# First head of an attention kernel prepared in two halves, with its hash bits in one bank

## The chip, the cores and the metric

The kernel runs on one core of a Trainium2 chip. The metric is the device time of the whole program in microseconds (us), the median of several executions. The engines are TensorE (PE in the rows, its weight loads PEld), VectorE (DVE), ScalarE (ACT), GpSimd (POOL) and SyncE (SP), which here only issues DMAs.

## The reference, cut to what matters

Four batches of eight heads, 768 positions, 64 values to a position. Six random projections give each query and key six sign bits; a query sees only the keys with the same bits. The result goes through a feed-forward layer of 3072 tokens.

```python
q_bits = (einsum('bhsd,dk->bhsk', q, proj) > 0); k_bits = (einsum('bhsd,dk->bhsk', k, proj) > 0)
q_bucket = sum(q_bits * 2**arange(6)); k_bucket = sum(k_bits * 2**arange(6))
scores = where(q_bucket == k_bucket, (q @ k.T) / sqrt(D), -1e9)
attn = exp(scores - max(scores)); attn = attn / (sum(attn) + 1e-9)
x = (attn @ v) reshaped to 3072 x 512
h = x @ w_in
g = where(h >= 1, h, where(h <= -1, 0, (h + 1)**2 / 4))
out = g @ w_out
```

## The kernel before

Every float32 operand is split into a rounded high part and the low remainder, each in an `fp32r` tile, and products are sums of matmuls over the parts. Two heads make a pair. Three buffers `T1[i]`, `T2[i]` hold a pair's q and k: high parts, low parts and, in eight rows of `T2`, the hash bits as large signed numbers (rows 0 to 6) and the negated, clamped row maxima (row 7), so that the score matmuls add mask and maximum by themselves. `sub` (L39) makes a low part: raw minus high.

Each of the 32 heads is 12 units `g` (two halves of the 768 queries by six blocks of 128 keys). A unit is two score matmuls (`s_unit`, L297 and L298), two exponentials on ScalarE (L306 rounded, L311 full), one subtraction for the low part `pl` (`lo_unit`; on GpSimd for key blocks 0 and 3, so in units 0, 3, 6 and 9 of a head, else on VectorE), and, four units later, three matmuls with v (`pv_unit`, L330 to L332). Beside them the maxima of a coming head are made: per block of 128 queries two matmuls into the one PSUM tile `smax` (`max_mm`, L258) and one reduce on VectorE (`max_red`, L262). As there is one such tile, TensorE and VectorE take it in turn. Then `max_clamp` (L269, L271), a transpose on TensorE (`max_tr`, L276), and `max_put`: a copy to `te` on ScalarE and two DMAs, into row 7 (L282) and into the scratch tensor `ed` (L283).

The bits of a coming pair come from four matmuls with the projection `pw` into an output bank (`bits_mm`, L178), a negated copy on ScalarE, a comparison on VectorE (`bits_cmp`, L189), a scaling on GpSimd (`bits_scale`, L221) and four DMAs (`bits_put`, L230). `move` (L157) copies q's and k's parts between partitions by DMA; `load_raw`, `load_v`, `cast_v` and `split_v` bring a pair's inputs and split v.

The order on each engine is the order of the code; `tasks[g]`, filled by `at(g, ...)`, holds the side work of unit g. Before unit 0 the first pair is prepared directly, without moves: `prep_direct` (L161 cast and four L39 subtractions on VectorE for head 0, on GpSimd for head 1, three copies on ScalarE), `bits_direct` (one bank, one negation and one comparison per half and per q or k), then `max_pre`, 12 score matmuls (L356) each with a reduce (L359). `keep_busy` puts matmuls into the program whose result nobody reads: 28 of them, 16 of 384 columns and 12 of 128.

## Time and profile before

| | us |
|---|---|
| median of three runs | 1021.12 (1020.1 to 1021.44) |
| profiled execution | 1021.61 |
| span in its trace | 1019.6 (2.0 lie around it) |
| TensorE busy in the span | 993.9 |
| VectorE, ScalarE, GpSimd busy | 696.6, 647.5, 395.0 |

A row of a timeline has start and duration in us, then engine, line, operation, tile written and tiles read; in brackets stands how long the engine had been idle and what released it. Tiles are given without their buffer number, so `t` stands for any part of `T1` or `T2`. "L258 of head 2" is the `max_mm` for the third head; it is the first work in the program that needs the second pair's tiles.

### The profile page before, as it was taken

What the parts mean: (1) busy time and instruction counts of PE and PEld (TensorE: products, weight loads), DVE (VectorE), ACT (ScalarE), POOL (GpSimd) and SP (SyncE); (2) the same over time, 40 slices, a digit from 0 to 9 for tenths busy, and PEclk for the clock granted to TensorE, in tenths of its full rate; (3) what the DMA queues carried; (4) which work ended last, traced back from release to release, by engine and by line L of the source; (5) the groups of instructions that cost most, each with busy time, mean ns of one, the idle gap of its engine ahead of it and who ended that gap; (6) DMA issues with size and microseconds to landing.
All of it is one profiled execution on the core that took longest, in us unless ns stands there. A gap on an engine that the chain in (4) does not pass through costs nothing.

```text
span 1019.6 us, 15241 instructions
## 1 busy us (share of the span) xinstructions
PE 993.9 (97%) x5180; PEld 917.5 (90%) x5180; DVE 696.6 (68%) x1108; ACT 647.5 (64%) x1430; POOL 395.0 (39%) x458
## 2 busy tenths in 40 slices
...
GB/s 89 167 110 155 160 171 174 182 169 169 158 171 153 152 141 144 127 107 180 63 80 88 50 32 79 47 22 81 24 77 48 1 79 47 32 71 24 32 1 32
DMA packets 52229, 99.06 MB, mean 97 GB/s; under 512 B 12856, under 2 KB 33976, under 8 KB 52152
## 3 DMA queue, kind: packets, MB, share of 16 engines
...
q14 instruction: 36, 0.29, 0.1%
q10 hardware_dynamic: 216, 0.00, 0.0%
...
## 4 chain that ended last, share of the span: by engine, by line
PE 89%; DVE 5%; ACT 2%; DMA 1%; issue 1%; SPq 0%; POOL 0%; DVEq 0%; ACTq 0%
PE y L638 26%; PE h L600 25%; PE smax L258 7%; PE o L332 6%; PE s L298 6%; PE o L330 6%; PE o L331 6%; PE s L297 6%; PE o L178 2%; DVE nm L262 1%; DMA wsq<-wd 1%; DVE nm L359 1%; DVE pl L39 0%; ACT ph L306 0%; DMA pj_raw<-in_pj_dram 0%
## 5 line engine op out<-in xcount | busy, mean ns | idle before, releaser
L607 DVE SCALAR_TENSOR_TENSOR t<-t 128x384 f32<-128x384 f32 x128 | 73.0, 571 | 257.6 <-ACT z L606 257.5
L605 ACT ACTIVATE t<-h,mh 128x384 f32<-128x384 f32 x128 | 74.3, 581 | 267.4 <-PE h L600 266.2
L306 ACT ACTIVATE ph<-s 128x384 fp32r<-128x384 f32 x380 | 188.1, 495 | 46.9 <-PE s L298 40.6
L262 DVE TENSOR_REDUCE nm<-smax 128x1 f32<-128x768 f32 x186 | 176.2, 947 | 19.9 <-PE smax L258 18.4
L39 POOL TENSOR_TENSOR pl<-pf,ph 128x384 fp32r<-128x384 f32 x128 | 137.9, 1083 | 81.2 <-ACT pf L311 80.8
L39 DVE TENSOR_TENSOR pl<-s,ph 128x384 fp32r<-128x384 f32 x256 | 135.5, 544 | 15.3 <-ACT s L311 14.0
L550 POOL TENSOR_TENSOR xraw<-xraw,xr 128x384 f32<-128x384 f32 x24 | 30.2, 1258 | 272.2 <-DVE xraw L547 272.2
L297 PE MATMUL s<-t 128*128 128x384 f32 x384 | 132.0, 344 | 0.8 <-DVE t L212 0.8
L332 PE MATMUL o<-pl,va 128*128 128x386 f32 x384 | 130.4, 339 | 0.4 <-DVE pl L39 0.3
L298 PE MATMUL s<-t 128*128 128x384 f32 x384 | 130.2, 339 | 0.0
L330 PE MATMUL o<-ph,va 128*128 128x386 f32 x384 | 130.1, 339 | 0.0
L331 PE MATMUL o<-ph,vb 128*128 128x386 f32 x384 | 129.5, 337 | 0.0
L311 ACT ACTIVATE s<-s 128x384 f32<-128x384 f32 x252 | 125.3, 497 | 0.0
L600 PE MATMUL h<-t,wih 128*128 128x384 f32 x480 | 122.7, 336 | 0.0
L638 PE MATMUL y<-t,ghi 128*128 128x512 f32 x384 | 120.2, 394 | 0.0
L258 PE MATMUL smax<-t 128*128 128x384 f32 x372 | 101.5, 353 | 5.4 <-DVE nm L262 4.5
L600 PEld LDWEIGHTS h<-t,wih 128*128 128x128 f32 x480 | 88.0, 188 | 4.9
L258 PEld LDWEIGHTS smax<-t 128*128 128x128 f32 x372 | 63.9, 188 | 22.1 <-DVE nm L262 21.1
L606 ACT ACTIVATE z<-t,m 128x384 f32<-128x384 f32 x128 | 79.0, 617 | 4.1
L638 PEld LDWEIGHTS y<-t,ghi 128*128 128x128 f32 x384 | 71.4, 188 | 11.2
L600 PE MATMUL h<-t,wil 128*128 128x384 f32 x240 | 80.8, 337 | 0.0
L638 PE MATMUL y<-t,glo 128*128 128x512 f32 x192 | 76.3, 398 | 2.9 <-DVE glo L627 2.9
...
## 6 DMA issues: line engine op xcount, KB each, us to landing
...
```

The lines of the kernel that those rows point to most:

```text
L39: eng.tensor_tensor(out=out, in0=a, in1=b, op=ALU.subtract)
L258: nc.tensor.matmul(out=smax[hd][:, hf, 0:HS], lhsT=t2[:, 0, h, i * P:(i + 1) * P], rhs=t2[:, 1, h, hf * HS:(hf + 1) * HS], start=True, sto ...
L262: nc.vector.tensor_reduce(out=nmp(hd)[:, i:i + 1], in_=smax[hd][:, :, 0:HS], axis=AX.XY, op=ALU.max, negate=True)
L297: nc.tensor.matmul(out=ps[:, 0:HS], lhsT=t1[:, 1, h, ks], rhs=t1[:, 0, h, sl], start=True, stop=False)
L298: nc.tensor.matmul(out=ps[:, 0:HS], lhsT=t2[:, 1, h, ks], rhs=t2[:, 0, h, sl], start=False, stop=True)
L306: nc.scalar.activation(out=ph[:, 0:HS], in_=ps[:, 0:HS], func=AF.Exp, scale=SCALE)
L311: nc.scalar.activation(out=pf, in_=ps[:, 0:HS], func=AF.Exp, scale=SCALE)
L330: nc.tensor.matmul(out=o, lhsT=wa, rhs=ph, start=(jj == 0), stop=False)
L331: nc.tensor.matmul(out=o, lhsT=wb, rhs=ph, start=False, stop=False)
L332: nc.tensor.matmul(out=o, lhsT=wa, rhs=pl, start=False, stop=(jj == NJ - 1))
L600: nc.tensor.matmul(out=ps[:, 0:CH], lhsT=w[:, cs], rhs=x[:, ct, :], start=(n == 0), stop=(n == 3 * NCT - 1))
L638: nc.tensor.matmul(out=ys[c][m], lhsT=g_[:, ms], rhs=w, start=(f == 0 and k == 0), stop=(f == NFT - 1 and k == 2))
```

## The change

The first head is cast, split and turned into bits in two halves of 384 columns, loaded by two DMAs (`hi_low`, `hi_copy`). q's and k's bits of a half lie in one bank (`direct_mm`), with one negation and one comparison for both on 40 rows. Head 1's raw data is loaded ahead of v. GpSimd's clearing of tiles stands first in its queue, but for T2[2], which it clears in unit 8. Eight of ten copies into `pw` go to units 1 and 2; `cast_v(0)` stands ahead of the exponentials. The first head's maxima are put in two halves (`half_max`, `half_clamp`, `half_put`). Eleven unread matmuls are left (five of 384 columns, six of 128). Head 1's maxima run in units 2 to 7 where they ran in 1 to 6; the second pair's bits are put in unit 9, behind `max_put`, where they were put in unit 8 ahead of it. In the changed kernel the lines are L305 and L306 for the score matmuls, L266 and L270 for the maxima, L284 for the transpose, L290 and L291 for `te` and L238 for the bits.

```diff
+    def hi_low(h, raw, eng, hf):
+        t1, t2 = T1[0], T2[0]
+        sl = slice(hf * HS, (hf + 1) * HS)
+        eng.tensor_copy(out=t2[:, 1, h, sl], in_=raw[:, sl])
+        sub(nc, eng, t1[64:128, 1, h, sl], raw[64:128, sl], t2[64:128, 1, h, sl].bitcast(F32))
+        sub(nc, eng, t1[0:64, 0, h, sl], raw[0:64, sl], t2[0:64, 1, h, sl].bitcast(F32))
+    def hi_copy(h, raw, sl, which):
+        t1, t2 = T1[0], T2[0]
+        out, rows = ((t1[0:64, 1], slice(64, 128)), (t1[64:128, 0], slice(0, 64)),
+                     (t2[64:128, 0], slice(0, 64)))[which]
+        nc.scalar.copy(out=out[:, h, sl], in_=raw[rows, sl])
...
+    def direct_mm(h, hf, ps):
+        direct[hf] = ps
+        sl = slice(hf * HS, (hf + 1) * HS)
         for t in (1, 0):
...
+            nc.tensor.matmul(out=ps[:, 0:HS], lhsT=pw[:, 3 - t, :], rhs=T1[0][:, t, h, sl],
+                             start=(t == 1), stop=(t == 0))
...
+    def direct_cmp(h, hf):
+        ps = direct[hf][0:40, 0:HS]
+        nc.vector.tensor_tensor(out=ps, in0=ps, in1=direct[h, "neg"][:, hf * HS:(hf + 1) * HS], op=ALU.is_gt)
+    def direct_scale(h, t, hf, eng):
+        rows = slice(0, 8) if t else slice(32, 40)
+        ps, out = direct[hf][rows, 0:HS], T2[0][0:8, t, h, hf * HS:(hf + 1) * HS]
...
+    def half_max(q, i, hf, ps):
+        t2 = T2[0]
+        n = q * HT + i
+        nc.tensor.matmul(out=ps[:, 0:HS], lhsT=t2[:, 0, 0, n * P:(n + 1) * P],
+                         rhs=t2[:, 1, 0, hf * HS:(hf + 1) * HS], start=True, stop=True)
+        return lambda: nc.vector.tensor_reduce(out=half[q][0][:, hf, i:i + 1], in_=ps[:, 0:HS], axis=AX.X,
+                                               op=ALU.max, negate=True)
+    def half_clamp(q):
+        a, nm = half[q]
+        nc.vector.tensor_reduce(out=nm[:, 0:HT], in_=a.rearrange("p f i -> p i f"), axis=AX.X, op=ALU.min)
...
+    def half_put(q, ps):
+        k = (1 + 2 * q) * HT
+        nc.tensor.transpose(out=ps[0:k, 0:P], in_=half[q][1], identity=ident)
+        te = small.tile([k, P], F32R, name=f"te{q}", bufs=1)
+        nc.scalar.copy(out=te, in_=ps[0:k, 0:P])
+        nc.sync.dma_start(out=T2[0][7:8, 0, 0, q * HS:(q + 1) * HS].bitcast(F32), in_=te[0:HT, :].bitcast(F32))
+        if q == 1:
+            nc.sync.dma_start(out=e_d[0][0:1, :], in_=te[HT:k, :].bitcast(F32))
...
+    for sl in (H0, H1):
+        nc.sync.dma_start(out=first[0][:, :, sl], in_=qk[0][:, 0:1, sl])
...
+    nc.sync.dma_start(out=first[1], in_=qk[0][:, 1:2])
     load_v(0)
-    nc.sync.dma_start(out=first[1], in_=qk[0][:, 1:2])
     load_raw(1)
-    nc.vector.memset(pw.bitcast(F32), 0.0)
-    nc.vector.memset(T2[0][0:64, 0].bitcast(F32), 0.0)
-    for i in (1, 2):
-        nc.gpsimd.memset(T2[i][0:64, 0].bitcast(F32), 0.0)
+    nc.vector.memset(pw[:, 2:4].bitcast(F32), 0.0)
+    nc.vector.memset(T2[0][0:64, 0, 0].bitcast(F32), 0.0)
     make_identity(nc, ident)
+    for t, x in [(t, 1.0) for t in VA] + [(t, 0.0) for t in VB]:
+        nc.gpsimd.memset(t[:, :, 1].bitcast(F32), x)
+    for t, x in [(t, 1.0) for t in PH] + [(t, 0.0) for t in PL]:
+        nc.gpsimd.memset(t[:, HS:HS + 2].bitcast(F32), x)
+    nc.gpsimd.memset(T2[0][0:64, 0, 1].bitcast(F32), 0.0)
+    nc.gpsimd.memset(pw[:, 0:2].bitcast(F32), 0.0)
+    nc.gpsimd.memset(T2[1][0:64, 0].bitcast(F32), 0.0)
     nc.scalar.copy(out=pj_hi, in_=pj_raw)
     nc.vector.tensor_tensor(out=pj_raw, in0=pj_raw, in1=pj_hi.bitcast(F32), op=ALU.subtract)
...
+    def pw_put(i, rows, c, low=32):
         nc.scalar.copy(out=pw[rows, i, c:c + NB], in_=pj_hi[rows].bitcast(F32))
-        nc.scalar.copy(out=pw[rows, i, 32 + c:32 + c + NB], in_=pj_raw[rows])
...
+    pw_put(2, slice(0, 128), 0, 64)
+    pw_put(3, slice(0, 128), 32, 64)
+    for hf, sl in ((0, H0), (1, H1)):
+        hi_low(0, raw, nc.vector, hf)
+        for n in range(2):
+            hi_copy(0, raw, sl, n)
+    hi_copy(0, raw, H0, 2)
+    spare = ps_m.tile([P, 2, 512], F32, name="smax")
+    for hf in range(2):
+        direct_mm(0, hf, spare[:, hf])
+        direct_neg(0, hf)
         keep_busy(HS)
+    keep_busy(HS)
+    keep_busy(HS)
+    direct_cmp(0, 0)
+    direct_scale(0, 1, 0, nc.vector)
+    direct_scale(0, 0, 0, nc.scalar)
+    direct_cmp(0, 1)
+    direct_scale(0, 1, 1, nc.scalar)
+    direct_scale(0, 0, 1, nc.scalar)
+    for hf in range(2):
+        hi_low(1, raw1, nc.gpsimd, hf)
+    hi_copy(0, raw, H1, 2)
+    for n in range(2):
+        hi_copy(1, raw1, slice(0, S), n)
     cast_v(0, nc.scalar)
-    for h in range(2):
-        split_v(0, nc.gpsimd, h)
+    for hf in range(2):
+        for n in range(3):
+            red = half_max(0, n, hf, bank())
+            keep_busy(P)
+            red()
+    half_clamp(0)
+    keep_busy(HS)
+    half_put(0, obank[0])
+    reds = [half_max(1, n, hf, bank()) for n in range(2) for hf in range(2)]
+    direct_mm(1, 0, obank[1])
+    direct_neg(1, 0)
+    direct_mm(1, 1, obank[0])
+    direct_neg(1, 1)
+    spare = ps_m.tile([P, 2, 512], F32, name="smax")
+    reds += [half_max(1, 2, hf, spare[:, hf]) for hf in range(2)]
+    for r in reds[0:4]:
+        r()
+    direct_cmp(1, 0)
+    direct_cmp(1, 1)
+    for r in reds[4:6]:
+        r()
+    half_clamp(1)
+    for hf in range(2):
+        direct_scale(1, 1, hf, nc.scalar)
+        direct_scale(1, 0, hf, nc.vector)
+    for n in range(2):
+        cast_h(1, nc.gpsimd, n, 0)
+        low_h(1, nc.gpsimd, n, 0)
+    split_v(0, nc.gpsimd, 0)
+    for n in range(2):
+        cast_h(1, nc.gpsimd, n, 1)
+        low_h(1, nc.gpsimd, n, 1)
+    split_v(0, nc.gpsimd, 1)
+    at(1, half_put, 1, ps_m.tile([P, 2, 512], F32, name="smax")[:, 0])
+    at(0, hi_copy, 1, raw1, slice(0, S), 2)
+    for n, p in enumerate(((0, slice(0, 64), 0), (0, slice(64, 128), 16), (1, slice(0, 64), 8),
+                           (1, slice(64, 128), 24))):
+        at(1 + n // 2, pw_put, *p)
+    at(8, nc.gpsimd.memset, T2[2][0:64, 0].bitcast(F32), 0.0)
     for n in range(3):
-        at(0, move, 1, n)
+        at(3, move, 1, n)
     for hf in range(2):
-        at(2 + 2 * hf, bits_mm, 1, hf, 1)
-        at(3 + 2 * hf, bits_cmp, 1, hf)
-    at(5, move, 1, 3)
-    at(6, bits_scale, 1, nc.gpsimd)
-    at(7, max_clamp, 1, nc.gpsimd)
-    at(8, bits_put, 1)
-    at(8, max_tr, 1, 1)
-    at(8, max_put, 1)
+        at(4 + 2 * hf, bits_mm, 1, hf, 1)
...
+        at(5 + 2 * hf, bits_cmp, 1, hf)
+    at(7, move, 1, 3)
+    at(8, bits_scale, 1, nc.gpsimd)
+    at(8, max_clamp, 1, nc.gpsimd)
+    at(9, max_tr, 1, None)
+    at(9, max_put, 1)
+    at(9, bits_put, 1)
     at(0, load_raw, 2)
     at(0, load_v, 1)
...
-            hd, i, due = 1, g - 1, 1 <= g <= NJ
+            hd, i, due = 1, g - 2, 2 <= g < 2 + NJ
```

On VectorE, at the preparation of the first head (`wraw` is the head's raw data, `t2_0` and `t1_0` the first pair's buffers), before:

```order
L386 TENSOR_TENSOR pj_raw_147<-pj_raw_147,pj_hi_148 128x6
L161 CAST t2_0_77<-wraw_168 128x768
L39 TENSOR_TENSOR t1_0_74<-wraw_168,t2_0_77 64x384 x4
L206 TENSOR_TENSOR s_209<-s_209,xs_208 8x384
L206 TENSOR_TENSOR s_215<-s_215,xs_207 8x384
L212 TENSOR_SCALAR t2_0_77<-s_209,cv8_146 8x384
L212 TENSOR_SCALAR t2_0_77<-s_215,cv8_146 8x384
L206 TENSOR_TENSOR s_212<-s_212,xs_208 8x384
L206 TENSOR_TENSOR s_218<-s_218,xs_207 8x384
L359 TENSOR_REDUCE nm2_237<-s_238 128x1
```

and now:

```order
L423 TENSOR_TENSOR pj_raw_147<-pj_raw_147,pj_hi_148 128x6
L163 CAST t2_0_77<-wraw_174 128x384
L39 TENSOR_TENSOR t1_0_74<-wraw_174,t2_0_77 64x384 x2
L163 CAST t2_0_77<-wraw_174 128x384
L39 TENSOR_TENSOR t1_0_74<-wraw_174,t2_0_77 64x384 x2
L213 TENSOR_TENSOR smax_231<-smax_231,xs_234 40x384
L221 TENSOR_SCALAR t2_0_77<-smax_231,cv2_146 8x384
L213 TENSOR_TENSOR smax_231<-smax_231,xs_234 40x384
L369 TENSOR_REDUCE nm20_168<-s_259 128x1
L369 TENSOR_REDUCE nm20_168<-s_263 128x1
```

The cast and the four subtractions became two casts of half the width with two subtractions each, and four comparisons became two.

On GpSimd at units 6 to 8 (`pl` are low parts of the exponentials, `raw` the third pair's inputs, `vb_1` the second pair's v, `bits` the second pair's), before:

```order
L39 TENSOR_TENSOR pl_3_164<-pf_406,ph_3_157 128x384
L221 TENSOR_SCALAR bits_399<-neg_400,cvt_145 32x768
L146 CAST t2_2_79<-raw_371 128x384
L39 TENSOR_TENSOR t1_2_76<-raw_371,t2_2_79 128x384
L39 TENSOR_TENSOR pl_6_167<-pf_451,ph_6_160 128x384
L269 TENSOR_SCALAR nm_389<-nm_389 128x6
L271 TENSOR_SCALAR nm_389<-nm_389 128x6
L146 CAST t2_2_79<-raw_371 128x384
L39 TENSOR_TENSOR t1_2_76<-raw_371,t2_2_79 128x384
L39 TENSOR_TENSOR vb_1_153<-vraw_373,va_1_151 128x6x64
```

and now:

```order
L39 TENSOR_TENSOR pl_3_164<-pf_376,ph_3_157 128x384
L146 CAST t2_2_79<-raw_340 128x384
L39 TENSOR_TENSOR t1_2_76<-raw_340,t2_2_79 128x384
L39 TENSOR_TENSOR pl_6_167<-pf_425,ph_6_160 128x384
L146 CAST t2_2_79<-raw_340 128x384
L39 TENSOR_TENSOR t1_2_76<-raw_340,t2_2_79 128x384
L39 TENSOR_TENSOR vb_1_153<-vraw_342,va_1_151 128x6x64
L564 MEMSET t2_2_79 64x1536
L229 TENSOR_SCALAR bits_404<-neg_405,cvt_145 32x768
L277 TENSOR_SCALAR nm_378<-nm_378 128x6
L279 TENSOR_SCALAR nm_378<-nm_378 128x6
```

The bits' scaling stood ahead of the unit's low part; now it stands behind two casts and subtractions, a piece of v and the clearing of `t2_2`, with the clamp right behind it.

On SyncE at units 8 and 9, before (`te` is head 1's maxima):

```order
L157 DMA t1_1_75<-t2_1_78 64x1536
L230 DMA t2_1_78<-bits_399 8x768 x4
L282 DMA t2_0_77<-te_494 1x6x128
L283 DMA ed0_67<-te_494 6x128
L157 DMA t2_2_79<-t2_2_79 64x1536
```

and now:

```order
L157 DMA t1_1_75<-t2_1_78 64x1536
L290 DMA t2_0_77<-te_491 1x6x128
L291 DMA ed0_67<-te_491 6x128
L238 DMA t2_1_78<-bits_404 8x768 x4
L157 DMA t2_2_79<-t2_2_79 64x1536
```

The two DMAs of the maxima now stand ahead of the four of the bits.

## Rows read from the trace of the kernel before

**Rows 1.** Windows: us, busy by engine (instructions), PEclk granted, DMA share, GB/s.
```profile
42.10:63.00 20.90, 19.48 (x97) 15.97 (x97) 16.70 (x23) 12.98 (x31) 9.54 (x14) 1.00 0.55 148
...
63.00:1019.60 956.60, 948.09 (x4963) 878.76 (x4961) 650.79 (x1033) 607.61 (x1338) 358.00 (x392) 1.00 0.36 95
```

**Rows 2.** Timeline of the first 9 us: start, duration, engine, line, operation, [idle <-releaser].
```profile
4.54 0.20 ACT L385 CAST pj_hi<-pj_raw 128x6 fp32r<-128x6 f32 x1 [1.00 <-DMA pj_raw<-in_pj_dram]
...
7.11 0.83 ACT L163 CAST t<-wraw 64x768 fp32r<-64x768 f32 x1
...
4.84 0.55 DVE L161 CAST t<-wraw 128x768 fp32r<-128x768 f32 x1
...
6.91 0.91 POOL L161 CAST t<-wraw 128x768 fp32r<-128x768 f32 x1 [3.00 <-DMA wraw<-in_qk_dram]
```

**Rows 3.** Tile t on VectorE, first 10 us; ns are least/median/most.
```profile
L39 DVE TENSOR_TENSOR t<-wraw,t x4: 551/553/1084, 5.4 to 7.1; 64x384 fp32r<-64x384 f32 x4
```

**Rows 4.** Timelines of VectorE and GpSimd near 94 us.
```profile
94.15 1.24 DVE L82 SCALAR_TENSOR_TENSOR wsq<-wsq,wa 128x512 f32<-128x512 f32 x1
...
94.78 0.97 POOL L146 CAST t<-raw 128x384 fp32r<-128x384 f32 x1
```

**Rows 5.** Groups by form, first 30 us: busy, mean ns | idle before, releaser.
```profile
L206 DVE TENSOR_TENSOR s<-s,xs 8x384 f32<-8x384 f32 x8 | 4.2, 549 | 2.7 <-ACT xs L200 2.7
...
L200 ACT ACTIVATE xs<-s 8x384 f32<-8x384 f32 x8 | 3.2, 469 | 0.0
...
L212 DVE TENSOR_SCALAR t<-s,cv 8x384 fp32r<-8x384 f32 x4 | 2.5, 658 | 0.0
...
L208 ACT ACTIVATE t<-s,cv 8x384 fp32r<-8x384 f32 x4 | 2.4, 655 | 4.0 <-DVE s L206 4.0
```

**Rows 6.** Timelines of TensorE and VectorE, first head's maxima.
```profile
12.06 0.66 PE L356 MATMUL s<-t 128*128 128x384 f32 x1 [2.42 <-DVE t L212]
...
17.39 0.39 PE L356 MATMUL s<-t 128*128 128x384 f32 x1
...
13.87 5.62 DVE L359 TENSOR_REDUCE nm<-s 128x1 f32<-128x384 f32 x11 [0.55 <-PE s L356]
```

**Rows 7.** Timelines of TensorE and VectorE, 45 to 47 us.
```profile
45.62 0.61 PE L258 MATMUL smax<-t 128*128 128x384 f32 x2 [0.17 <-DVE nm L262]
...
46.26 0.96 DVE L262 TENSOR_REDUCE nm<-smax 128x1 f32<-128x768 f32 x1 [0.24 <-PE smax L258]
```

**Rows 8.** Page, section 5: costliest groups, mean ns of one second.
```profile
L311 ACT ACTIVATE s<-s 128x384 f32<-128x384 f32 x252 | 125.3, 497 | 0.0
```

**Rows 9.** Timeline of GpSimd, start and 34 to 38 us.
```profile
0.71 2.69 POOL L383 MEMSET t<- 64x1536 f32 x2 [0.29 <-POOLq L840]
...
34.39 0.97 POOL L221 TENSOR_SCALAR bits<-neg,cvt 32x768 fp32r<-32x768 f32 x1 [2.66 <-DVE neg L189]
35.32 0.49 POOL L146 CAST t<-raw 128x384 fp32r<-128x384 f32 x1
...
36.87 1.01 POOL L39 TENSOR_TENSOR pl<-pf,ph 128x384 fp32r<-128x384 f32 x1
37.84 0.24 POOL L269 TENSOR_SCALAR nm<-nm 128x6 f32<-128x6 f32 x1
```

**Rows 10.** Timelines of TensorE and SyncE, 35 to 43 us.
```profile
38.46 0.28 PE L276 MATMUL o<-ident,nm 128*12 128x128 f32 x1 [0.74 <-POOL nm L271]
...
42.10 0.52 PE L258 MATMUL smax<-t 128*128 128x384 f32 x2
...
35.39 3.25 SPq L230 DMA_DIRECT2D t<-bits  x4
39.05 0.72 SPq L282 DMA_DIRECT2D t<-te  x1
39.82 0.46 SPq L283 DMA_DIRECT2D ed<-te  x1
```

**Rows 11.** DMA from 35 to 40 us in 40 slices of 0.125 us.
```profile
GB/s 49 492 246 0 98 492 197 0 0 131 0 0 0 25 123 25 25 0 0 0 0 0 0 98 74 0 90 0 74 49 49 25 0 0 98 74 0 25 0 0
```

More of the change, by code (lines that the diff above doesn't have):

```diff
@@ new lines, in direct_mm, with direct_neg @@
+            nc.tensor.matmul(out=ps[:, 0:HS], lhsT=pw[:, 3 - t, :], rhs=T1[0][:, t, h, sl],
+                             start=(t == 1), stop=(t == 0))
+    def direct_neg(h, hf):
+        if (h, "neg") not in direct:
+            direct[h, "neg"] = work.tile([P, S + 2], F32, name="xs")[0:40]
+        nc.scalar.activation(out=direct[h, "neg"][:, hf * HS:(hf + 1) * HS], in_=direct[hf][64:104, 0:HS],
+                             func=AF.Copy, scale=-1.0)
+    def direct_cmp(h, hf):
+        ps = direct[hf][0:40, 0:HS]
+        nc.vector.tensor_tensor(out=ps, in0=ps, in1=direct[h, "neg"][:, hf * HS:(hf + 1) * HS], op=ALU.is_gt)
@@ L216, in bits_scale @@
+    def direct_scale(h, t, hf, eng):
+        rows = slice(0, 8) if t else slice(32, 40)
+        ps, out = direct[hf][rows, 0:HS], T2[0][0:8, t, h, hf * HS:(hf + 1) * HS]
+        if eng is nc.scalar:
+            eng.activation(out=out, in_=ps, func=AF.Identity, scale=cv2[rows, 0:1], bias=cv2[rows, 1:2])
+        else:
+            eng.tensor_scalar(out=out, in0=ps, scalar1=cv2[rows, 0:1], scalar2=cv2[rows, 1:2],
+                              op0=ALU.mult, op1=ALU.add)
     def bits_scale(pr, eng):
@@ L274, in max_tr @@
     def max_tr(hd, bank):
-        ps = mx[hd] = obank[bank]
+        ps = mx[hd] = ps_m.tile([P, 2, 512], F32, name="smax")[:, 0] if bank is None else obank[bank]
         nc.tensor.transpose(out=ps[0:2 * NJ, 0:P], in_=nms.pop(hd), identity=ident)
@@ L347, in keep_busy @@
         nc.tensor.matmul(out=obank[1][:, 0:n], lhsT=pw[:, 2], rhs=T2[0][:, 1, 0, 0:n], start=True, stop=True)
-    def max_pre(hd):
-        pr, h = hd // 2, hd % 2
-        t2 = T2[pr % NQK]
-        nm = small.tile([P, 2, NJ], F32, name="nm2")
-        for i in range(NJ):
-            for hf in range(2):
-                sm = ps_s.tile([P, 512], F32, name="s")
-                nc.tensor.matmul(out=sm[:, 0:HS], lhsT=t2[:, 0, h, i * P:(i + 1) * P],
-                                 rhs=t2[:, 1, h, hf * HS:(hf + 1) * HS], start=True, stop=True)
-                keep_busy(P)
-                nc.vector.tensor_reduce(out=nm[:, hf, i:i + 1], in_=sm[:, 0:HS], axis=AX.X,
-                                        op=ALU.max, negate=True)
-        for _ in range(9):
-            keep_busy(HS)
-        nc.vector.tensor_reduce(out=nmp(hd)[:, 0:NJ], in_=nm.rearrange("p f i -> p i f"), axis=AX.X, op=ALU.min)
+    HT = NJ // 2
@@ new lines, in attention @@
+    half = [(small.tile([P, 3, HT], F32, name=f"nm2{q}", bufs=1),
+             small.tile([P, (1 + 2 * q) * HT], F32, name=f"nmh{q}", bufs=1)) for q in range(2)]
+    for a, _ in half:
+        nc.vector.memset(a[:, 2], CLAMP)
+    def half_max(q, i, hf, ps):
[5 more added lines that the diff above has]
+                                               op=ALU.max, negate=True)
@@ L365, in raw0, with bank @@
+    def bank():
+        return ps_s.tile([P, 512], F32, name="s")
     def raw0():
```

69 lines of the change are left out of this document (10 added, 59 removed).

## Prediction

> **What bounds the kernel now.** I read the windows first, to find where TensorE is not the limit, then the engines' timelines there. From 63 us to the end TensorE is busy 948.09 of 956.60 us at a granted clock of 1.00 [rows 1]: with the same code there, that stretch can only be moved, not shortened. From 42.1 to 63 us it is busy 19.48 of 20.90 us, and what paces it is the one `smax` tile: L258 begins every 1.66 us or so, released by VectorE's reduce L262, which in turn waits for L258 [rows 7]. The code there is the same too. So the change is worth what it does to one moment: the first L258 of head 2, at 42.10 us before [rows 10]. It needs the second pair's bits, and these come at the end of a chain through everything that the change touches: preparation of head 0, maxima of head 0, head 1's maxima, GpSimd's scaling and clamp, and a DMA. I work that chain out step by step; about 0.05 us is allowed from one engine to the next.
>
> **The change part by part.** (a) *Preparation of head 0.* VectorE can't start before the projection: `pj_raw` lands at 4.5 us and VectorE's cast begins at 4.84 us [rows 2]. Both stay, so the smaller and earlier loads of head 0 give nothing. Before, a cast of 0.55 and four subtractions followed, in all to 8.2 us. After, the first half needs a cast of 0.35 (an estimate between half of 0.55 and the whole) to 5.2 and a subtraction of 0.55 to 5.8.
>
> Now GpSimd comes in. Its queue holds first the clearing: a 64x1536 memset takes 1.37 each (2.69 for two [rows 9]); one such, half of one, the ends of `va`, `vb`, `ph`, `pl` and half of `pw`, with the identity, I add up to 5.6 us from a start at 0.71. Then it casts and subtracts head 1, whose data now comes ahead of v and should land by then; before, it waited for it until 6.91 [rows 2]. The row that decides is VectorE's subtraction: of four, the median took 553 ns and one 1084 [rows 3], the one beside GpSimd's 6.91 cast. Near 94 us it shows again on both sides: a VectorE operation on two tiles took 1.24 us and GpSimd's cast behind it 0.97 [rows 4] against 0.49 alone [rows 9]. So I let the two engines take turns: VectorE's second subtraction ends at 6.6, GpSimd's subtraction at 7.5, VectorE's second cast at 7.7, GpSimd's next at 8.55, VectorE's third subtraction at 8.95 and its fourth at 9.75. Without turns it would be 7.65. Both ends stay for the range.
>
> Then a serial chain, as L213 waits for the negation and the scalings wait for one another: bits matmuls 0.65 (by the 0.66 of the 128x384 matmul at 12.06 [rows 6]), negation 0.47, comparison 0.55, scaling on VectorE 0.66 and on ScalarE 0.65 [rows 5]: 9.8 + 2.98 + handovers of 0.3 = 13.05 us for the first L367, where L356 began at 12.06. The four negations and four comparisons that are saved, on 8 rows, were not on that chain: before, the second half's were done beside the first half's maxima. The 40-row ones are taken at the same price, since rows lie across partitions (8x384 and 128x384 both take some 0.5 [rows 3, 5]).
>
> (b) *Maxima of head 0.* Six reduces at 0.51 (5.62 for eleven [rows 6]) after a matmul of 0.65 end at 16.95, the clamp at 17.15. The next four reduces wait for the transpose and a matmul behind it: 17.2 + 0.3 + 0.65, then 4 x 0.51 to 20.25. Head 1's first comparison ends at 20.85. Its scalings on ScalarE take 2 x 0.65 to 22.2; behind them in ScalarE's queue stand two pairs of exponentials, 0.75 a pair (by starts; one is 0.497 long [rows 8]), with a 0.83 copy between them [rows 2] and the `te` copy of 0.25. This last must be read out before head 1's maxima can have the `smax` tile: 22.2 + 0.75 + 0.83 + 0.75 + 0.25 = 24.8 us for the first L266.
>
> (c) *Head 1's maxima and GpSimd's list.* Pairs follow at 1.66, 1.66 and 1.95 us (the last with head 1's bits in the same bank of work), so the scores of unit 6 come at about 30.4 and its exponentials are out at 31.85. GpSimd takes its low part then, 0.97, and must work off in order what stands behind: a cast and a subtraction (1.55), a piece of v (0.97), the clearing of T2[2] (1.35), the scaling (0.93), the two clamps (0.56) [rows 9]: 6.33 in all, to 38.2 us. TensorE's transpose L284 follows at 38.25, where L276 began at 38.46 [rows 10]. On the way TensorE is two units further in the heads than it would otherwise be, but that is work which is paid for anyway.
>
> (d) *From the transpose to head 2.* Transpose 0.3 and `te` copy 0.25 end at 38.85. SyncE issues L290 (0.77 to the next start), L291 (0.5) and the first bits DMA (0.81, a quarter of 3.25 [rows 10]); the second, which head 2 needs, starts at 40.95. Before, the bits DMAs were issued from 35.39, ahead of `te`. The first of them moved data until about 37.25 [rows 11], 1.9 us behind its issue; with 2.0 the second lands at 42.95. So L266 of head 2 stands at 42.95 against 42.10: 0.85 us late. By the profiled execution that is 1021.61 + 0.85 = 1022.46; the median of the runs is 0.49 below that execution, so 1021.97.
>
> *At no price:* the unread matmuls taken out (TensorE waits where they stood), eight `pw` copies moved into units 1 and 2 (hidden while VectorE works on the halves; without that cover at most the 1.5 us between ScalarE's 4.54 row and its long copies, which end with the one at 7.11 [rows 2]), and v's split, some 8 us earlier by this sum but awaited by nobody. `move(1)` in units 3 and 7 is issued some 10 us before head 2 reads its data.
>
> **The rivals.** *The clearing holds up the cast.* VectorE's cast at 4.84 might not run beside GpSimd's memsets, and begin at 5.6 instead. In the trace GpSimd stood idle at that time [rows 2], so no row excludes it. The first half then ends at 6.0 and 6.6, the turns come out one later: 1.25 more, 1023.2 us. It decides if the first cast isn't done by 5.3. The Trainium skill's page "SBUF — State Buffer", section "Who interferes with whom", says that copies and casts in VectorE's two-port modes exclude GpSimd for the whole instruction, and that a subtraction with both inputs in SBUF collides only with GpSimd instructions that read; by this the memset would block the cast and the turns of (a) would be right. The 1084 ns row agrees with the second part; no row here shows the first.
>
> *Slower: TensorE falls back to its lower clock.* Seventeen unread matmuls are gone. The granted clock reads 1.00 in all windows [rows 1], yet the same 128x384 matmul took 0.66 at 12.06 and 0.39 at 17.39 [rows 6], so TensorE did speed up on the way, in a stretch that was densely filled. Between 17 and 25 us the changed kernel has gaps of 1 to 3 us. If TensorE is at 1.2 GHz after these, a unit's five matmuls and the pair of maxima cost 7 x 0.33 = 2.3 us against the pace of 1.66 [rows 7]; three such units make 2.0 us: 1024.0. It decides if L305 stays above 0.5 us each beyond 25 us.
>
> *Faster: no turns.* If the two engines don't hinder one another in head 0's preparation, 2.1 us go out of (a), and VectorE's scalings in (b) beside GpSimd's casts need no allowance either, some 0.5 more, if they are what the `te` copy waits for: 1021.97 - 2.6 = 1019.4. For it speaks that three of four subtractions took 0.55; against it, that GpSimd was idle during those three.
>
> *The change does not do what it says* would be that the halves bring no earlier start; that is part of the forecast already.
>
> **How the numbers follow.** Forecast, 1022.0: 0.39. Clearing holds up the cast, 1023.2: 0.20. Lower clock, 1024.0: 0.21. No turns, 1019.4: 0.20. The chain has some forty terms, so each of these has a width of about 1.2 us either way. What a measurement of this kernel can tell from no change is 0.2%, 2.04 us: faster is below 1019.1, slower above 1023.2. Below 1019.1 lie nearly half of the last case (0.09), a little of the forecast (0.03) and what I allow for a chain that is shorter than worked out in (c), where GpSimd's list may not be what is last (0.08): 0.20. Above 1023.2 lie half of the second case (0.10), most of the third (0.15) and some of the forecast (0.05): 0.30. The rest is 0.50. From 1018.2 to 1024.8 the four cases lie but for 2 in 10; the range takes in both ends of the turns (1019.9 without) and of the clock.
>
> **What would show it.** VectorE's last subtraction of head 0 ends at about 9.75 (7.65 without turns, 10.95 if the cast was held up); the first L367 starts at about 13.05, the first L266 at 24.8, L284 at 38.25, released by GpSimd's L279, and L266 of head 2 at 42.95, released by the bits' DMA; from there all starts are later by one and the same amount, and the windows behind it are as long as before. The prediction is wrong if L284 is released by something else, if the DMA from `bits` takes other than 2 us, or if TensorE's matmuls beyond 25 us take other times than before.

## The result, and the profile after

The changed kernel takes 1023.58 us (median of seven runs, 1021.42 to 1025.16) where the kernel before takes 1021.09: a ratio of 1.0025, 95% interval 1.0015 to 1.0035. It is slower by about 2.5 us. The forecast was 1022.0 and the range 1018.2 to 1024.8; the sign of the difference was forecast, the size was 0.9 us of the measured 2.5. The time lies in the range, but above 1023.2, where the prediction had put 0.30 of its chance.

The profiled execution happened to be the shortest of the seven, 1021.42 us with a span of 1019.1. I therefore had the unchanged program profiled once more (`again` below): 1026.02 us, span 1023.9, the longest of its twelve. The two traces bracket the kernel, and both are read here.

The chain of the prediction is there, step by step. From the timelines of GpSimd and TensorE, first trace (start, duration, engine, line, operation, tiles, [idle before, releaser]); these answer [rows 9] and [rows 10]:

```profile
31.43 1.01 POOL L39 TENSOR_TENSOR pl<-pf,ph 128x384 fp32r<-128x384 f32 x1 [2.34 <-ACT pf L319]
...
37.52 0.23 POOL L279 TENSOR_SCALAR nm<-nm 128x6 f32<-128x6 f32 x1
...
23.61 0.61 PE L266 MATMUL smax<-t 128*128 128x384 f32 x2 [0.91 <-ACT te L385]
...
37.81 0.38 PE L284 MATMUL smax<-ident,nm 128*12 128x128 f32 x1 [2.37 <-POOL nm L279]
...
43.07 0.59 PE L266 MATMUL smax<-t 128*128 128x384 f32 x2 [0.80 <-DMA t<-bits]
```

GpSimd takes unit 6's low part at 31.43, works off its list, and ends the second clamp at 37.75. L284 had waited 2.37 us for it ("<-POOL nm L279"). Head 2's L266 waited 0.80 for the bits' DMA and starts at 43.07, where L258 started at 42.10 with no wait. The second trace has the same two waits, later:

```profile
33.72 1.01 POOL L39 TENSOR_TENSOR pl<-pf,ph 128x384 fp32r<-128x384 f32 x1 [3.96 <-ACT pf L319]
...
40.11 0.28 PE L284 MATMUL smax<-ident,nm 128*12 128x128 f32 x1 [2.37 <-POOL nm L279]
...
45.32 0.83 PE L266 MATMUL smax<-t 128*128 128x384 f32 x2 [1.78 <-DMA t<-bits]
```

What the traces also have, and the trace of before has not behind 20 us, is half clock. The windows of the changed kernel, first trace and then second (columns as in [rows 1], granted clock in the third from last):

```profile
24.20:27.60 3.40, 2.90 (x10) 2.38 (x9) 2.38 (x3) 2.85 (x10) 1.07 (x2) 0.50 0.95 271
...
37.80:41.20 3.40, 3.39 (x12) 3.40 (x13) 0.56 (x1) 1.80 (x5) 3.23 (x5) 0.51 0.01 2
...
63.00:1019.10 956.10, 948.39 (x4967) 880.95 (x4965) 648.94 (x1035) 608.73 (x1340) 359.55 (x393) 1.00 0.35 95
```

```profile
25.00:31.80 6.80, 6.22 (x20) 5.84 (x19) 4.30 (x6) 4.07 (x13) 2.46 (x3) 0.50 0.93 247
...
45.50:48.90 3.40, 3.40 (x12) 3.40 (x12) 1.50 (x2) 1.28 (x3) 0.51 (x1) 0.50 0.90 202
...
63.00:1023.90 960.90, 952.47 (x4983) 883.60 (x4981) 652.76 (x1038) 610.58 (x1346) 361.52 (x394) 1.00 0.35 95
```

In these stretches TensorE is nearly always busy, at 1.2 GHz. In the first trace the second stretch lies ahead of the wait for the bits, which it only shortens. In the second trace the first stretch is twice as long and lies in head 1's maxima, and the second lies behind the arrival of the bits, where TensorE is the limit. Behind 63 us the changed kernel takes 956.1 and 960.9 us where it took 956.6 [rows 1]; the cuts don't lie at the same unit, and counted from head 2's first score matmul to that of the last unit of the attention, the first trace takes 407.7 us, the second 408.7 and the trace of before 409.1. So executions with one program differ by about 1 us there too. A third stretch at half clock, near 485 us in both traces of the changed kernel, lies behind the attention and shows no price: from the last unit to the end they take 549.0 us, the trace of before 549.2.

### The profile page after: what moved, and what is told of

Same layout as the page of the kernel before. It is cut to its first block, busy times and chain, and to the rows that moved or that the text cites. A ratio compares the mean times of both kernels' runs of the same rounds, so it can differ in the third digit from the quotient of the medians.

```text
span 1019.1 us, 15219 instructions
## 1 busy us (share of the span) xinstructions
PE 995.6 (98%) x5164; PEld 921.0 (90%) x5164; DVE 691.8 (68%) x1107; ACT 648.7 (64%) x1433; POOL 397.2 (39%) x461
## 4 chain that ended last, share of the span: by engine, by line
PE 89%; ACT 3%; DVE 3%; POOL 1%; DMA 1%; issue 1%; SPq 1%; ACTq 0%; POOLq 0%; DVEq 0%
PE y L717 26%; PE h L679 26%; PE smax L266 7%; PE s L306 6%; PE o L340 6%; PE o L338 6%; PE s L305 6%; PE o L339 6%; PE o L181 2%; DVE nm L270 2%; POOL t L39 1%; ACT ph L314 1%; DMA wraw<-in_qk_dram 1%; ACT s L319 0%; ACT va L245 0%
## 5 line engine op out<-in xcount | busy, mean ns | idle before, releaser
L314 ACT ACTIVATE ph<-s 128x384 fp32r<-128x384 f32 x380 | 188.2, 495 | 47.2 <-PE s L306 39.7
L270 DVE TENSOR_REDUCE nm<-smax 128x1 f32<-128x768 f32 x186 | 176.4, 949 | 22.3 <-PE smax L266 20.6
L39 POOL TENSOR_TENSOR pl<-pf,ph 128x384 fp32r<-128x384 f32 x128 | 140.5, 1102 | 91.0 <-ACT pf L319 90.7
L305 PE MATMUL s<-t 128*128 128x384 f32 x384 | 133.0, 346 | 0.0
L306 PE MATMUL s<-t 128*128 128x384 f32 x384 | 131.3, 342 | 0.0
L266 PE MATMUL smax<-t 128*128 128x384 f32 x372 | 100.8, 352 | 5.4 <-DVE nm L270 3.0
L266 PEld LDWEIGHTS smax<-t 128*128 128x128 f32 x372 | 64.8, 189 | 20.1 <-DVE nm L270 17.5
```

Source lines behind the costliest of these rows:

```text
L39: eng.tensor_tensor(out=out, in0=a, in1=b, op=ALU.subtract)
L266: nc.tensor.matmul(out=smax[hd][:, hf, 0:HS], lhsT=t2[:, 0, h, i * P:(i + 1) * P], rhs=t2[:, 1, h, hf * HS:(hf + 1) * HS], start=True, sto ...
L270: nc.vector.tensor_reduce(out=nmp(hd)[:, i:i + 1], in_=smax[hd][:, :, 0:HS], axis=AX.XY, op=ALU.max, negate=True)
L305: nc.tensor.matmul(out=ps[:, 0:HS], lhsT=t1[:, 1, h, ks], rhs=t1[:, 0, h, sl], start=True, stop=False)
L306: nc.tensor.matmul(out=ps[:, 0:HS], lhsT=t2[:, 1, h, ks], rhs=t2[:, 0, h, sl], start=False, stop=True)
L314: nc.scalar.activation(out=ph[:, 0:HS], in_=ps[:, 0:HS], func=AF.Exp, scale=SCALE)
```

## The experiments

Theory A is that of the prediction: one chain sets head 2's L266, and the time follows it. Its rival, theory B, is that TensorE's clock falls in the waits and takes time on top. All kernels are variants of the changed one, but for `before_few`; each ratio is to the kernel before, which ran in turn with it. `again` is the changed kernel itself. `again`, `memset_start`, `long_first` and `early_list` ran in one round, the others in two later ones without the changed kernel; where their ratios are set against its 1.0026, the difference carries both intervals, some 1.4 us.

> The changed kernel itself, once more, to see a second trace of it. In its first trace the first L266 of head 2 began at 43.07 us against 42.10 before, yet the span was 0.5 us shorter than before's, while the median of seven runs was 2.5 us longer. Theory A (the chain alone): L266 of head 2 is again at 43.0 to 43.2, and what is beyond 1 us in the median comes after it. Theory B (TensorE's clock): the trace has stretches of half clock again, in the waits near 24 and 38 us and near 485 us, and the executions that are longer have one more of them, each worth up to 1.7 us where TensorE is the limit. Both: the ratio to before stays between 1.001 and 1.004.

Measured: 1023.18 us, ratio 1.0026 (1.0016 to 1.0036). Head 2's L266 came at 45.32, not at 43.1: theory A alone fails. The lateness grows in three steps: 0.7 us in the first head's preparation (first L367 at 12.49, first trace 11.80), 1.6 in head 1's maxima at half clock (GpSimd's unit 6 at 33.72, 2.3 later), and 1.5 behind 45.5.

**The start.** `memset_start` puts the clearing of T2[2] back to the start:

```diff
     nc.gpsimd.memset(T2[1][0:64, 0].bitcast(F32), 0.0)
+    nc.gpsimd.memset(T2[2][0:64, 0].bitcast(F32), 0.0)
...
-    at(8, nc.gpsimd.memset, T2[2][0:64, 0].bitcast(F32), 0.0)
```

> The clearing of T2[2] goes from unit 8 back to GpSimd's queue at the start, behind the clearing of T2[1], where GpSimd was idle until 7.37 us. Theory A: GpSimd's list ahead of the clamp is 1.37 us shorter, so L284 moves from 37.81 to 36.4 and L266 of head 2 from 43.07 to 41.7; the time falls by 1.4 us. Theory B: the gap ahead of L284 is shorter (1.0 for 2.4 us), so a half-clock stretch may go too; then it falls by up to 3 us. Rival C (GpSimd's list is not what is last): L284 stays near 37.8.

Measured: 1025.73, ratio 1.0046 (1.0035 to 1.0058): 2 us slower where 1.4 faster was expected. The timelines of VectorE and GpSimd, this kernel:

```profile
4.10 2.83 DVE L163 CAST t<-wraw 128x384 fp32r<-128x384 f32 x1
6.97 2.00 DVE L39 TENSOR_TENSOR t<-wraw,t 64x384 fp32r<-64x384 f32 x2
...
10.08 2.02 DVE L39 TENSOR_TENSOR t<-wraw,t 64x384 fp32r<-64x384 f32 x2
...
5.34 1.37 POOL L422 MEMSET t<- 64x1536 f32 x1
...
7.38 2.45 POOL L39 TENSOR_TENSOR t<-wraw,t 64x384 fp32r<-64x384 f32 x2
```

and the same of the changed kernel, first trace, with a row of ScalarE:

```profile
4.10 1.51 DVE L163 CAST t<-wraw 128x384 fp32r<-128x384 f32 x1
5.64 1.14 DVE L39 TENSOR_TENSOR t<-wraw,t 64x384 fp32r<-64x384 f32 x2
6.71 0.34 DVE L163 CAST t<-wraw 128x384 fp32r<-128x384 f32 x1
7.08 1.33 DVE L39 TENSOR_TENSOR t<-wraw,t 64x384 fp32r<-64x384 f32 x2
...
4.02 1.38 POOL L421 MEMSET t<- 64x1536 f32 x1
7.37 0.63 POOL L163 CAST t<-wraw 128x384 fp32r<-128x384 f32 x1 [1.98 <-DMA wraw<-in_qk_dram]
...
3.79 0.20 ACT L422 CAST pj_hi<-pj_raw 128x6 fp32r<-128x6 f32 x1
```

VectorE's cast begins at 4.10 in both and ends just behind GpSimd's clearing, at 5.61 and at 6.93; the second cast, 0.34 us, has nothing beside it. Held up until 6.93, VectorE then meets GpSimd's work on head 1 with everything it has left: 2.00 and 2.02 us for pairs of subtractions that take 1.14 alone. The list did become shorter as expected: from GpSimd's unit 6 at 36.41 to L284 at 41.48 it is 5.1 us instead of 6.4, and L284's wait fell from 2.37 to 1.06. Only the start lost more, 3.7 us to the first L367 (15.46; 3.0 against the second trace).

`long_first` asks whether short clearings let the cast in between:

```diff
+    nc.gpsimd.memset(T2[1][0:64, 0].bitcast(F32), 0.0)
     make_identity(nc, ident)
...
-    nc.gpsimd.memset(T2[1][0:64, 0].bitcast(F32), 0.0)
```

> The 64x1536 clearing of T2[1] goes from the end of GpSimd's clearing to its front, so that short ones stand beside VectorE's first cast. In the changed kernel that cast took 1.51 us from 4.10 and ended 0.2 behind the long clearing, and 0.34 in the second half. If the clearing blocked it: the cast ends by 4.8 instead of 5.6, head 0's chain is 0.8 to 1.1 us earlier (first L367 at 10.8 instead of 11.80) and, as units 0 to 6 follow one another, L284 is near 36.9 and L266 of head 2 near 42.1. If the cast waited for its data (the load of head 0): it still ends near 5.6 and nothing moves.

Measured: 1023.37, ratio 1.0024 (1.0015 to 1.0033), no change. VectorE and GpSimd:

```profile
4.10 1.50 DVE L163 CAST t<-wraw 128x384 fp32r<-128x384 f32 x1
...
3.98 0.28 POOL L419 MEMSET ph<- 128x2 f32 x7
...
4.40 0.73 POOL L420 MEMSET t<- 64x768 f32 x1
5.08 0.31 POOL L421 MEMSET pw<- 128x256 f32 x1
```

The cast ends at 5.60 again, though only shorter clearings stood beside it, sixteen from 3.98 to 5.39: it waits for the whole row of them. The first L367 came at 13.28, later than in either trace of the changed kernel, since GpSimd had head 1's data at 6.29 and the last two subtractions took 2.53 us beside its work. Whether the cast waits for GpSimd or for its data is told apart by `free_start`, where nothing of GpSimd's is left at 4.1:

```diff
-    nc.sync.dma_start(out=first[1], in_=qk[0][:, 1:2])
     load_v(0)
+    nc.sync.dma_start(out=first[1], in_=qk[0][:, 1:2])
...
     nc.vector.memset(T2[0][0:64, 0, 0].bitcast(F32), 0.0)
+    nc.vector.memset(T2[1][0:64, 0].bitcast(F32), 0.0)
...
-    nc.gpsimd.memset(T2[1][0:64, 0].bitcast(F32), 0.0)
```

> Only the start of the changed kernel is altered: VectorE clears T2[1] itself while it waits for the projection, so GpSimd's clearing ends near 4.1 us, and v is loaded ahead of head 1's raw data, so GpSimd's casts and subtractions of head 1 fall behind VectorE's preparation of head 0. If the blocked cast and the turns with GpSimd are what makes that preparation long: VectorE's cast takes 0.35 from 4.10, its four subtractions end near 7.2 (8.4 and 9.1 in two traces of the changed kernel), the first L367 starts near 10.4 (11.80 and 12.5), and L284 and head 2's L266 come 1.3 to 2 us earlier; the time falls by 1.3 to 2 us against the changed kernel unless TensorE's clock takes it back. If the cast waited for data, the start stays as it is.

VectorE and TensorE:

```profile
4.07 0.35 DVE L163 CAST t<-wraw 128x384 fp32r<-128x384 f32 x1
4.46 1.14 DVE L39 TENSOR_TENSOR t<-wraw,t 64x384 fp32r<-64x384 f32 x2
...
5.90 1.14 DVE L39 TENSOR_TENSOR t<-wraw,t 64x384 fp32r<-64x384 f32 x2
9.25 0.56 DVE L213 TENSOR_TENSOR smax<-smax,xs 40x384 f32<-40x384 f32 x1 [2.21 <-ACT xs L208]
...
11.33 0.69 PE L367 MATMUL s<-t 128*128 128x384 f32 x1 [1.68 <-ACT t L219]
...
38.60 0.28 PE L284 MATMUL smax<-ident,nm 128*12 128x128 f32 x1 [2.37 <-POOL nm L279]
```

The cast takes 0.35 and the subtractions end at 7.04, so it was GpSimd that the cast waited for. The time is 1022.37, ratio 1.0009 (1.0000 to 1.0018): by the ratios 1.7 us less than the changed kernel, within the expected 1.3 to 2, but with an uncertainty nearly as large. The trace doesn't show the expected path to it: L284 at 38.60 and head 2's L266 at 43.81 lie between the two traces of the changed kernel, as two stretches at half clock (22.6 to 29.4 and 39.7 to 43.1) stand on the way. The first L367, at 11.33, gains less than VectorE, because ScalarE's copies and negations are then what is late (L213 at 9.25 waited 2.21 us for L208). L284 waits the same 2.37 us for the same list.

**The clock.** `before_few` takes 17 of the 28 unread matmuls out of the kernel before:

```diff
-                keep_busy(P)
+                if hf == 0:
+                    keep_busy(P)
...
-        for _ in range(9):
+        for _ in range(5):
...
-    for _ in range(7):
-        keep_busy(HS)
```

> The kernel before, with as few unread matmuls as the changed one: 5 for 9 behind the first head's maxima, none for 7 behind head 1's bits, 6 for 12 beside the maxima. Theory B (the clock falls where unread matmuls are missing): the trace shows half clock somewhere between 17 and 50 us, head 2's L258 comes 1 us or more later than 42.10, and the time rises by 1 to 2 us. Theory A: TensorE waits there anyway, the clock stays at 1.00, no change.

A window and a row of TensorE:

```profile
25.00:31.80 6.80, 6.28 (x19) 5.20 (x18) 4.44 (x8) 5.57 (x12) 3.25 (x4) 0.50 0.97 247
...
42.53 0.52 PE L258 MATMUL smax<-t 128*128 128x384 f32 x2
```

Measured: 1021.47, ratio 0.9996 (0.9987 to 1.0005). Half clock appears at once, and the time doesn't move, so neither theory's expectation came out whole. Head 2's L258 started at 42.53, 0.43 us later than before [rows 10]. The first unit was 0.07 us later (24.09 against 24.02), so 0.36 us is what 6.8 us at half clock left on this chain. In the kernel before, head 1's pairs stand further apart, up to 2.7 us, and most of the loss goes into TensorE's waits.

In the changed kernel the pairs stand closer. `warm` and `warm2` put unread matmuls into its waits:

```diff
+    def unread(n):
+        ps = ps_s.tile([P, 512], F32, name="s")
+        for _ in range(n):
+            nc.tensor.matmul(out=ps[:, 0:HS], lhsT=T2[0][:, 0, 0, 0:P], rhs=T2[0][:, 1, 0, 0:HS], start=True, stop=True)
+    at(0, unread, 4)
+    at(1, unread, 3)
+    at(2, unread, 2)
+    for _ in range(10):
+        at(9, keep_busy, HS)
```

`warm` also has five in place of two `keep_busy(HS)` ahead of `direct_cmp(0, 0)`, so 22 more in all, not 21.

> The changed kernel with 21 more unread matmuls of 384 columns, in its waits: three behind head 0's bits, four, three and two in units 0, 1 and 2, ten ahead of L284 in unit 9, where TensorE waited 2.4 us. Theory B (the clock): no stretch of half clock is left between 20 and 50 us, head 2's L266 comes at 43 us in every execution instead of up to 4 us later, and the median falls by 1.5 to 2.5 us against the changed kernel, with a smaller spread. Theory A (the chain alone): head 2's L266 stays at 43.1 or gets later by the unread matmuls' own time (up to 1 us), and the median doesn't fall.

> The changed kernel with 19 unread matmuls of 384 columns in the waits of units 0, 1, 2 and 9, and none more ahead of unit 0, where three of them held up the first L367 by some 0.7 us in the run before. Theory B: no half clock between 20 and 50 us, pairs L266 of head 1 follow at 1.7 us throughout, head 2's L266 near 43.1, median 1 to 2 us below the changed kernel's. Theory A: median as the changed kernel's.

`warm2`, TensorE and then windows:

```profile
24.42 0.61 PE L266 MATMUL smax<-t 128*128 128x384 f32 x2 [0.38 <-ACT te L385]
26.08 0.62 PE L266 MATMUL smax<-t 128*128 128x384 f32 x2 [0.35 <-DVE nm L270]
...
38.00 0.28 PE L284 MATMUL smax<-ident,nm 128*12 128x128 f32 x1 [0.60 <-POOL nm L279]
...
43.22 0.59 PE L266 MATMUL smax<-t 128*128 128x384 f32 x2 [1.77 <-DMA t<-bits]
```

```profile
20.00:44.20 24.20, 19.49 (x102) 16.97 (x101) 15.24 (x26) 17.10 (x44) 18.03 (x23) 1.00 0.48 124
44.20:47.60 3.40, 3.40 (x12) 3.40 (x11) 1.81 (x3) 1.37 (x4) 0.00 (x0) 0.50 0.98 228
```

`warm2`: 1022.45, ratio 1.0009 (0.9999 to 1.0019). The first pairs follow at 1.66 and 1.67 us, the clock is whole until 44.2, and by the ratios 1.7 us of the 2.6 are gone, give or take 1.4, though one stretch is left where the expectation had none: behind a wait of 1.77 us for the bits. `warm` measured 1024.36, ratio 1.0033 (1.0021 to 1.0045), no better than the changed kernel, though its trace has no half clock between 20 and 480 us: theory B's expectation failed there. Its three further matmuls stand on the chain (first L367 at 13.22, against 12.60 in `warm2`). That is 0.6 us; the other 1.3 between the two medians are not explained.

The traces price half clock with less noise. From the first L367 to head 2's L266 it is 30.7 us in `warm` and 30.6 in `warm2`, where the clock is whole on the way, 31.3 in the changed kernel's first trace, 32.5 in `free_start` and 32.8 in the second trace: 0.6 to 2.2 us on the chain. What is left behind 44 us cost `warm2` 1.0 us over the next three units (5.6 for 4.6). The record has the mean granted clock of each execution as well: of the changed kernel's 19, the eight at 0.993 have a median of 1024.9 us, the eleven at 0.994 or 0.995 one of 1023.0. That goes together; it doesn't show by itself which causes which, and the six executions of `warm`, at 0.996 to 1.000, took 1022.5 to 1025.1.

**The list.** `early_list` scales in unit 7, clamps on VectorE and puts the bits in unit 8, issues the `te` row's DMA from ScalarE, and clears T2[2] at the start as in `memset_start`:

```diff
+        (nc.scalar if hd == 1 else nc.sync).dma_start(out=T2[pr % NQK][7:8, 0, h, :] ...
...
-    at(8, bits_scale, 1, nc.gpsimd)
-    at(8, max_clamp, 1, nc.gpsimd)
+    at(7, bits_scale, 1, nc.gpsimd)
+    at(8, max_clamp, 1, nc.vector)
+    at(8, bits_put, 1)
...
-    at(9, bits_put, 1)
```

> On top of the clearing at the start: the bits' scaling in unit 7 ahead of that unit's cast, the clamp on VectorE, the bits' DMAs in unit 8 and the te row's DMA on ScalarE's queue. Theory A: the scaling follows the comparison at 33.6, the bits' second DMA lands near 37.2, the clamp follows the last reduce at 34.7, L284 runs without a wait near 35.6 and L266 of head 2 near 38.7; the time falls by 4.4 us against the changed kernel and by 3.3 us against the kernel before. Theory B agrees, with up to 1.7 us more where a half-clock stretch disappears. Rival: the third pair's work on GpSimd, which now stands behind the scaling, is needed soon enough to give it back, and L266 of head 2 is early but the time is not.

Measured: 1023.94, ratio 1.0030 (1.0019 to 1.0041). Its start is that of `memset_start` (first L367 at 15.47), and against that kernel head 2's L266 came at 44.46 instead of 46.70, with half as long a stretch at half clock ahead of it. The 4.4 us weren't there: L284 still waited 1.86 us, now for VectorE's clamp. `best` has the same list on the start of `free_start`, with T2[2] cleared in unit 10; `best_warm` has the unread matmuls of `warm` as well, but three in unit 9 in place of ten (15 in all):

> The altered start of free_start, and the earlier list: bits' scaling in unit 7 ahead of that unit's cast, clamp on VectorE, bits' DMAs in unit 8, the te row's DMA on ScalarE's queue, T2[2] cleared in unit 10. With both: first L367 near 10.4, L284 without a wait near 34, head 2's L266 near 37.5 (43.07 in the changed kernel), 4.6 us ahead of the kernel before: about 1016.5 us. If half-clock stretches remain in the waits between 15 and 25 us, up to 1.7 us each come on top: up to 1020.

> The former with 14 unread matmuls in its waits (three behind head 0's bits, four, three and two in units 0 to 2, three ahead of L284 less one that the clock may not need). Theory B: granted clock 1.00 from 20 to 50 us, and up to 1.7 us faster than the former for each half-clock stretch that goes. Theory A: no faster than the former, slower by up to 1 us.

VectorE, GpSimd and TensorE of `best_warm`:

```profile
34.94 0.91 DVE L277 TENSOR_SCALAR nm<-nm 128x6 f32<-128x6 f32 x1
35.88 0.92 DVE L279 TENSOR_SCALAR nm<-nm 128x6 f32<-128x6 f32 x1
...
34.81 1.01 POOL L39 TENSOR_TENSOR t<-raw,t 128x384 fp32r<-128x384 f32 x1
35.77 1.00 POOL L39 TENSOR_TENSOR vb<-vraw,va 128x384 fp32r<-128x384 f32 x1
...
36.95 0.27 PE L284 MATMUL smax<-ident,nm 128*12 128x128 f32 x1 [1.35 <-DVE nm L279]
...
40.66 0.51 PE L266 MATMUL smax<-t 128*128 128x384 f32 x2
```

`best`: 1020.10, ratio 0.9990 (0.9981 to 0.9999). `best_warm`: 1019.22, ratio 0.9977 (0.9969 to 0.9986); it is the fastest, 2.2 us below the kernel before and, by the two ratios, 5 below the changed one. Both fall short of the 1016.5 expected of `best`. Two reasons show. The first L367 is at 11.35 in `best` where 10.4 was expected, as in `free_start`. And the clamp's two small operations take 0.91 and 0.92 us on VectorE beside GpSimd's two subtractions, where they take 0.24 each on GpSimd [rows 9], so L284 still waits 1.35 (1.85 in `best`). Head 2's L266 starts without a wait at 40.66. The trace of before already had such a pair, beside GpSimd and alone, in the first head's clamp on VectorE (GpSimd's subtraction ends at 20.52):

```profile
19.72 0.82 DVE L269 TENSOR_SCALAR nm<-nm 128x6 f32<-128x6 f32 x1
20.58 0.17 DVE L271 TENSOR_SCALAR nm<-nm 128x6 f32<-128x6 f32 x1
...
19.52 1.00 POOL L39 TENSOR_TENSOR t<-raw,t 128x384 fp32r<-128x384 f32 x1
```

`early_only` and `best2` return the clamp to GpSimd, ahead of the third pair's work, which moves one unit later (its moves too):

```diff
-    at(8, bits_scale, 1, nc.gpsimd)
+    at(7, bits_scale, 1, nc.gpsimd)
     at(8, max_clamp, 1, nc.gpsimd)
+    at(8, bits_put, 1)
...
+                gn = g0 + n + (pr == 0 and n > 0)
+                at(gn, cast_h, pr + 2, nc.gpsimd, n % 2, n // 2)
```

> The changed kernel with the list alone mended, the start as it is: bits' scaling in unit 7 ahead of the casts, the clamp next on GpSimd in unit 8, then the third pair's casts and v's split one unit later, bits' DMAs in unit 8, the te row on ScalarE's queue, T2[2] cleared in unit 10. If GpSimd's list and the order of the DMAs are what head 2 waits for: the wait of 2.4 us ahead of L284 goes, L284 is near 35.4 and head 2's L266 near 39.5 in an execution like the changed kernel's first trace (43.07), some 3.5 us less; with a clock at half in the waits of units 0 to 2, up to 2 us of it are lost. If not, the time stays at the changed kernel's.

> Altered start, mended list and 11 unread matmuls in units 0, 1, 2 and 9: first L367 near 11.35, L284 near 34.5 (36.95 with the clamp on VectorE, where two scalings of 128x6 took 0.91 and 0.92 beside GpSimd's casts), head 2's L266 near 38.4 against 40.66: 2 us below best_warm, so 1017 us, 3.9 below the kernel before. If the bits' or the te row's DMA is then what is late, 1018 to 1019.

TensorE and SyncE of `early_only`:

```profile
36.30 0.28 PE L284 MATMUL smax<-ident,nm 128*12 128x128 f32 x1
...
41.02 0.51 PE L266 MATMUL smax<-t 128*128 128x384 f32 x2
...
48.38 1.60 SPq L141 DMA_DIRECT2D raw<-in_qk_dram  x1
...
53.01 8.98 SPq L238 DMA_DIRECT2D t<-bits  x4
62.10 0.73 SPq L290 DMA_DIRECT2D t<-te  x1
...
63.93 0.69 PE L306 MATMUL s<-t 128*128 128x384 f32 x1 [3.35 <-DMA t<-te]
```

The first part came out: L284 has no wait, and head 2's L266 starts at 41.02 though the start was as in `again` (first L367 12.53), where it started at 45.32; in `best2` at 39.17. Then both give it back at head 2's first unit. The third pair's moves and, behind them, the loads now come later, the four bits' DMAs of that pair take 8.98 us to issue instead of 2.83 in `best_warm`, the `te` row behind them is issued at 62.10, and L306 waits 3.35 us (1.89 in `best2`). Half clock follows, from 63.1 to 69.9, and together they cost 5.9 us: head 2's seventh unit begins 12.8 us behind its first, where the changed kernel takes 6.9. So 1023.31, ratio 1.0016 (1.0003 to 1.0030), and 1019.77, 0.9992 (0.9978 to 1.0006). Of the twelve executions of `best2` the eight with a mean clock of 0.997 or more took 1018.3 to 1021.0, the four with less 1022.5 to 1024.7. A version with the clamp of `best2` and the moves of `best_warm` wasn't run.

## Why the prediction was right, and where it was not

| step (us) | forecast | first trace | second trace |
|---|---|---|---|
| VectorE's cast begins | 4.84 | 4.10 | 4.10 |
| its last subtraction ends | 9.75 | 8.41 | 9.12 |
| first L367 | 13.05 | 11.80 | 12.49 |
| first L266 | 24.8 | 23.61 | 24.30 |
| GpSimd's low part of unit 6 | 31.85 | 31.43 | 33.72 |
| L284 | 38.25 | 37.81 | 40.11 |
| L266 of head 2 | 42.95 | 43.07 | 45.32 |

*What bounds the kernel*: right. Both releasers named (L279 for L284, the bits' DMA for head 2's L266) are those of the traces, and from head 2's L266 on the first trace is later by 1.0 to 1.1 us at every pair up to 65 us, by one and the same amount as forecast. `early_only` moves head 2's start by mending one link, `best_warm` the time by mending three. But two of the prediction's own three signs of being wrong came: the bits' DMA took 2.5 us for 2, and TensorE's matmuls beyond 25 us took 0.52 us for 0.34 in the stretches at half clock.

*(a)* had two errors against each other. That the projection lands at 4.5 us and stays was wrong: ScalarE's first copy begins at 3.79, right behind its table load, without a wait. And the cast was not let through: 1.51 us for 0.35, which is the mechanism of the first rival, with 0.41 of delay against the forecast's 5.2 since all began 0.74 earlier. The turns were real but smaller than forecast, as head 1's data landed at 7.37 and 6.90, not by 5.6: the last two subtractions took 1.33 and 2.02 us, 1.14 alone. So earlier data of head 1 made head 0 later: with GpSimd at it from 7.37, 6.90 and 6.29 (`long_first`), VectorE's last subtraction ended at 8.41, 9.12 and 9.91. From L367 to the first L266 the forecast was 11.75, the traces have 11.81 and 11.81.

*(c)*: the list was forecast at 6.33 and took 6.32 in the first trace. The step that failed is the one ahead of it: the pairs at 1.66, 1.66 and 1.95. In the first trace unit 6's low part came 7.82 after the first L266, in the second 9.42, where 7.05 was forecast. That is half clock: in `warm2`, with the clock whole there, the pairs come at 1.66, 1.67 and 2.03 and the low part after 7.20. I had it as a rival with 0.21 and 2.0 us. On the chain the traces give it 0.6 to 2.2 us, so the rival was right in kind and size, and not an alternative to the forecast but a part of it. That all windows of the trace of before read 1.00 [rows 1] was no sign for the changed kernel: with 11 of its 28 unread matmuls `before_few` reads 0.50 from 25.0 to 31.8.

*(d)*: 4.70 forecast, 5.26 and 5.21 measured. The second bits' DMA landed some 2.5 us behind its issue, not 2.0.

*At no price*: the unread matmuls were not free to drop in the changed kernel, though in the kernel before they are, to within 0.1% (`before_few`). The reason given, that TensorE waits where they stood, holds for the time they take and leaves out the clock they keep.

That the first trace's head 2 starts at 43.07, with 42.95 forecast, is luck: 1.25 us won at the start were lost again by half clock (0.8 up to unit 6) and the DMA (0.6). Executions like the second trace, later by 2.3 us there and by 3.8 us a few units on, are why 1023.58 was measured and not 1022.0.

One term stayed open. Behind head 2's start the forecast was that nothing changes. From head 2's first unit to the last of the attention the traces of the kernel before and of `before_few` take 409.1 and 409.2 us, those of the changed kernel and of its variants 407.6 to 408.8 (without `early_only` and `best2`, whose third pair comes later). So some 1 us seems to be won there, and no run shows what wins it.
